# Two loads and two outputs cut in halves, PSUM pairs of any two banks, and new hand lists in a kernel of linear attention and a long convolution

## The chip, the cores and the metric

The kernel runs on one core of a Trainium2 chip. The core has a matrix engine (TensorE, PE in the profile, with its weight loads shown apart as PEld), a vector engine (VectorE, DVE), a scalar engine (ScalarE, ACT), GpSimd (POOL) and SyncE (SP), which here only issues DMAs. Each engine works through its own instructions in order, and waits on semaphores for the others. The accumulator memory PSUM has 8 banks of 512 fp32 numbers per partition. The metric is the device time of one execution in microseconds (us). Before the change three runs took 230.34, 230.67 and 233.8 us, median 230.67 us.

## The reference

The output is two results side by side, 2048 rows of 448 columns each. The left half is linear attention with 16 heads of width 28; the right half is a long convolution, done with Fourier transforms:

```python
# left half
q, k, v = split(x @ wqkv)                         # 2048 x 448 each, 16 heads
phi_q = [softmax(q @ w_phi), softmax(-(q @ w_phi))]   # per head; phi_k the same
kv = phi_k^T @ v;  z = sum(phi_k)
o = (phi_q @ kv) / (phi_q @ z + 1e-6);  a = o @ wo
# right half
K[d, l] = Re sum_n C[d,n] * exp(dt*A[d,n]*l) * dt*B[d,n]     # 448 x 2048, 256 states
y = irfft(rfft(pad(u)) * rfft(pad(K)))[:2048] + u * Dskip
```

## The kernel before, in words

The convolution is made of matrix products. `signal_spectrum(b)` (L417, twice) takes 1024 rows of `u` to the frequency side: it reverses rows with two pairs of matmuls, adds and subtracts on VectorE, and then runs eight groups of eight matmuls against the transform matrix `G1` (L437). Each group fills two PSUM banks, and one copy (L440) takes both banks out in one access. `tables(qt)` (L806) builds, for one quarter `qt` of the 448 channels, the powers of the states: `rotations` are sines on ScalarE, `dampings` are exponentials on ScalarE, both read from a PSUM pair that `args` (four accumulated products of 112 columns) has filled; `hi_tables`, `damp` and `far` are VectorE work; `build_k` (L573) makes the kernel's values with many small matmuls of 80 columns, four steps per bank; `scatter_k` sends them through DRAM. `kernel_spectrum(qt)` (L722) transforms them, and `conv(qt)` (L742) multiplies spectra on VectorE (`prod`), combines them with VectorE (`finish`) or, for two of the eight blocks, with matmuls (`finish_pe`), and `inverse(b, S)` (L781) returns to the time side: for each parity `r` of the rows 36 matmuls of 112 columns into one bank, a copy of 128x448, and a store of 112 KB. 16 such outputs exist.

The attention half is `fold_weights` (L396: `w_phi` folded into the query and key weights, from the loaded block `Wqk`), `key_side`, and `query_side(sc)` (L645) for each 512 rows: logits into four banks, exponentials on ScalarE, the sums, and then 32 matmuls that fill four banks, which two copies of 128x1024 empty (a pair of banks each); four output products of 512 rows follow. The load of `u`, `x`, the state matrices (`Are, Aim, Bre, Cre, Bim, Cim`, 229 KB each) and the weights stands at L283 to L312.

Nothing is scheduled at run time. Every operation is recorded, and four hand lists at the file's end decide all: `ORDER` is the order in which the recorded operations are issued (each engine and each DMA queue keeps that order), `PLACES` gives the SBUF place of each buffer, `SLOTS` the PSUM bank or pair of banks of each job, and `PICKS` the engine of each copy (A is ScalarE, V VectorE) and the queue of each DMA (S is SP's, Q ScalarE's). The semaphore waits are put in when the program is built, from the memory regions that the operations touch.

A pair of banks is read by one access with a stride:

```python
    def two(bs, parts=128):
        return view(psum[0:parts, bs[0], 0:1], [512 * (bs[1] - bs[0]), 2], [1, D_MODEL])
```

All helpers record through one line each, so the profile knows them by these: matmuls L229, PE transposes L239, VectorE tensor operations L186, activations L206 (a new function table is loaded before a sine or an exponential when the other was in use, L203 or L206), copies L214, DMAs L249 and transposing DMAs L245.

Of the kernel before, what the change touches and what calls it, by code (L numbers as in the profile page):

```python
# [17 lines left out]
D_MODEL = 448  # L18
# [111 lines left out]
def kernel(  # L130
# [28 lines left out]
    prog = Prog()  # L159
# [138 lines left out]
    Wqk = sb([112, 4, 2 * D_MODEL])  # L298
    WV = sb([128, 4, D_MODEL])
    dma("S", Wqk, wq3[:, :, 0:2 * D_MODEL])  # L300
# [8 lines left out]
    G1 = sb([128, 2, 4, 512])  # L309
    dma("S", G1, G_d)  # L310
    load_u(0)
# [84 lines left out]
    def fold_weights(which):  # L396
        for cp in range(2):
            p = bank16(*prog.banks(1), [112, 2, D_MODEL])
            c0 = which * D_MODEL + 224 * cp
            transposes([(p[:, k, 112 * j:112 * j + 112], Wqk[:, j, c0 + 112 * k:c0 + 112 * k + 112], id112)  # L400
                        for k in range(2) for j in range(4)])
            copy(wT[:, which, 2 * cp:2 * cp + 2, :], p)
# [14 lines left out]
    def signal_spectrum(b):  # L417
# [9 lines left out]
        for cp in range(2):  # L427
            for st in range(2):
                k = 2 * cp + st
                sg = sb([128, 4, 4, 112])  # L430
                for mp in range(2):
                    items = []
                    bs = prog.banks(2)
                    for k2 in range(2):
                        mt = 2 * mp + k2
                        items += acc(psum[:, bs[k2], 0:D_MODEL],
                                     [(G1[:, cp, jt, 128 * mt:128 * mt + 128], ab[:, cp ^ st, jt, :])  # L437
                                      for jt in range(4)])
                    mms(items)
                    copy(sg[:, :, 2 * mp:2 * mp + 2, :].rearrange("p g k x -> p k g x"),  # L440
                         two(bs).rearrange("p k (g x) -> p k g x", g=4))
# [300 lines left out]
    def conv(qt):  # L742
# [38 lines left out]
        def inverse(b, S):  # L781
            for r in range(2):
                (bk,) = prog.banks(1)
                items = []
                for jt in range(4):
                    items += acc(psum[:, bk, 112 * jt:112 * jt + 112],
                                 [(GI[:, r, cp, mt, 128 * jt:128 * jt + 128], S[:, r, cp, 112 * mt:112 * mt + 112])
                                  for cp in range(2) for mt in range(4)] + [(UT[:, b, r, 128 * jt:128 * jt + 128], DD[:, qt, :])])
                mms(items)
                OB = sb([128, 4, 112])  # L790
                copy(OB.rearrange("p t x -> p (t x)"), psum[:, bk, 0:D_MODEL])
                dma("S", rows(out2, b, r, D_MODEL + 112 * qt), OB)
# [89 lines left out]
).split()]  # L882
PLACES = [64 * int(i) for i in (
# [51 lines left out]
```

## Time and profile before

| | us |
|---|---|
| runs before: lowest, median, highest | 230.34, 230.67, 233.8 |
| the profiled execution, its own time | 231.53 |
| its span (first to last instruction in the trace) | 229.8 |
| TensorE busy | 200.5 (87%) |
| VectorE busy | 211.7 (92%) |
| ScalarE busy | 192.5 (84%) |
| GpSimd busy | 8.0 (3%) |
| mean granted TensorE clock | 0.985 |

The span is the time from the first to the last event on the core; the execution's own time is 1.73 us longer. Busy shares are means over the whole run: in the first ten microseconds the engines wait for loads, in the last eighty ScalarE is no longer full. So the shares are read by stages (a view that gives each engine's busy time in chosen stretches), and the waits beside them. A row of the timeline reads: start, length, engine, line, operation, destination and source with their shapes, how many instructions were joined into the row, and in brackets the idle time before it and what ended it. In the rows of instructions by form the numbers behind the bar are total busy time, the mean of one in nanoseconds, and the idle time before them.

### The profile page before, as it was taken

What the parts mean: (1) busy time and instruction counts of PE and PEld (TensorE: products, weight loads), DVE (VectorE), ACT (ScalarE), POOL (GpSimd) and SP (SyncE); (2) the same over time, 40 slices, a digit from 0 to 9 for tenths busy, and PEclk for the clock granted to TensorE, in tenths of its full rate; (3) what the DMA queues carried; (4) which work ended last, traced back from release to release, by engine and by line L of the source; (5) the groups of instructions that cost most, each with busy time, mean ns of one, the idle gap of its engine ahead of it and who ended that gap; (6) DMA issues with size and microseconds to landing.
All of it is one profiled execution on the core that took longest, in us unless ns stands there. A gap on an engine that the chain in (4) does not pass through costs nothing.

```text
span 229.8 us, 7332 instructions
## 1 busy us (share of the span) xinstructions
PE 200.5 (87%) x3126; PEld 145.6 (63%) x3136; DVE 211.7 (92%) x269; ACT 192.5 (84%) x351; POOL 8.0 (3%) x26
## 2 busy tenths in 40 slices
PE   1154589999999899999887999999999999999993
PEld 1052246655557565787754868565676977799993
DVE  1499999999999899998999999999999989997991
ACT  2799999999999999999999999999798978235320
POOL 2000000001003000020100000010000000000000
PEclk9999599999999999999999999999999999999999
DMA  6992860969638999965576402414949863658842
GB/s 164 187 226 61 239 157 2 222 146 148 163 95 227 196 204 225 170 129 119 179 184 78 161 0 86 161 53 25 289 92 255 276 152 51 73 28 113 232 93 61
DMA packets 77608, 32.87 MB, mean 143 GB/s; under 512 B 64792, under 2 KB 75656, under 8 KB 77192
## 3 DMA queue, kind: packets, MB, share of 16 engines
q1 hardware_dynamic: 69864, 30.11, 60.0%
q10 hardware_dynamic: 7712, 2.31, 5.1%
q8 instruction: 24, 0.39, 0.7%
q14 instruction: 8, 0.07, 0.1%
HBM read 15.84 MB, written 8.49 MB: 106 GB/s over the span
## 4 chain that ended last, share of the span: by engine, by line
ACT 30%; DVE 27%; PE 24%; issue 8%; DMA 8%; DVEq 0%; ACTq 0%
PE psum L229 24%; DVE sbuf L186 24%; ACT sbuf L206 17%; ACT sbuf L214 10%; DMA sbuf<-in_B_C_re_dram 3%; DMA sbuf<-sbuf 2%; DVE sbuf L214 2%; DMA sbuf<-const 2%; DMA sbuf<-in_B_log_dt_dram 1%; ACT L203 1%; ACT L206 1%; ACT sbuf L220 1%; DVE sbuf L198 0%; DVE sbuf L217 0%; DVEq L186 0%
## 5 line engine op out<-in xcount | busy, mean ns | idle before, releaser
L229 PE MATMUL psum<-sbuf 128*128 128x112 bf16 (+9 forms) x3078 | 198.7, 256 | 25.1 <-DVE sbuf L186 12.7
L186 DVE TENSOR_TENSOR sbuf<-sbuf 128x896 bf16<-128x896 bf16 (+13 forms) x214 | 190.2, 947 | 8.9 <-ACT sbuf L206 3.8
L229 PEld LDWEIGHTS <-sbuf 128*128 128x128 bf16 (+5 forms) x3088 | 142.9, 112 | 78.6 <-issue 20.8
L214 ACT CAST sbuf<-psum 128x448 bf16<-128x448 f32 (+6 forms) x122 | 78.6, 701 | 24.8 <-PE psum L229 24.0
L206 ACT ACTIVATE sbuf<-psum 128x512 bf16<-128x512 f32 (+6 forms) x154 | 82.5, 628 | 2.3 <-PE psum L229 1.4
L206 ACT ACTIVATE sbuf<-sbuf 128x896 bf16<-128x896 bf16 (+3 forms) x29 | 18.9, 691 | 2.1 <-DMA sbuf<-in_B_log_dt_dram 1.2
L214 DVE CAST sbuf<-psum 128x448 bf16<-128x448 f32 (+3 forms) x21 | 13.3, 644 | 2.4 <-PE psum L229 2.4
L206 ACT ACTIVATE sbuf<-psum,sbuf 128x896 f32<-128x896 f32 (+3 forms) x17 | 13.9, 833 | 0.0
L224 POOL MEMSET sbuf<- 128x224 bf16 (+7 forms) x21 | 7.6, 397 | 144.0 <-PE psum L229 77.4
L214 ACT COPY sbuf<-psum 112x896 bf16<-112x896 bf16 (+2 forms) x11 | 7.0, 662 | 1.8 <-PE psum L239 1.8
L203 ACT ACT_TABLE_LOAD x5 | 6.4, 1283 | 1.6 <-PEq L919 1.3
L206 ACT ACT_TABLE_LOAD x4 | 5.1, 1283 | 1.8 <-DVE sbuf L186 1.7
L239 PEld LDWEIGHTS <-sbuf 112*112 112x112 bf16 (+1 forms) x48 | 3.1, 120 | 2.0 <-issue 1.7
L239 PE MATMUL psum<-sbuf 112*112 112x112 bf16 (+1 forms) x48 | 3.7, 216 | 0.7 <-DVE sbuf L186 0.6
L186 DVE TENSOR_TENSOR sbuf<-psum,sbuf 128x448 bf16<-128x448 f32 (+1 forms) x6 | 2.9, 489 | 0.6 <-PE psum L229 0.6
L214 DVE CAST sbuf<-sbuf 128x1792 bf16<-128x1792 f32 (+1 forms) x4 | 2.7, 696 | 0.5 <-ACT sbuf L206 0.5
L214 DVE COPY sbuf<-sbuf 128x448 bf16<-128x448 bf16 (+2 forms) x12 | 2.9, 261 | 0.0
L217 DVE TENSOR_SCALAR sbuf<-sbuf 128x1568 bf16<-128x1568 bf16 (+1 forms) x5 | 2.7, 547 | 0.0
L214 ACT COPY sbuf<-sbuf 128x224 bf16<-128x224 bf16 (+2 forms) x6 | 2.5, 424 | 0.0
L220 ACT ACTIVATE sbuf<-sbuf 128x1792 f32<-128x1792 f32 x1 | 1.8, 1795 | 0.0
L198 DVE SCALAR_TENSOR_TENSOR sbuf<-sbuf,psum 128x128 f32<-128x128 f32 x4 | 1.1, 282 | 0.1
L198 DVE SCALAR_TENSOR_TENSOR sbuf<-sbuf 128x896 f32<-128x896 f32 x1 | 1.1, 1079 | 0.0
(8 smaller groups left out, 1.9 us busy)
## 6 DMA issues: line engine op xcount, KB each, us to landing
SUd<-sbuf SPq DMA_DIRECT2D x8, 448.0 KB, 3.6
sbuf<-SUd SPq DMA_DIRECT2D x4, 896.0 KB
sbuf<-const SPq DMA_DIRECT2D x3, 1024.0 KB, 6.0
sbuf<-const SPq DMA_DIRECT2D x8, 384.0 KB, 4.0
sbuf<-in_B_u_dram SPq DMA_DIRECT2D x4, 448.0 KB
out_dram<-sbuf SPq DMA_DIRECT2D x10, 112.0 KB
out_dram<-sbuf SPq DMA_DIRECT2D x2, 448.0 KB, 2.8
out_dram<-sbuf ACTq DMA_DIRECT2D x2, 448.0 KB
```

The source lines that it names most:

```text
L186: prog.add("V", lambda: nc.vector.tensor_tensor(out=o, in0=a, in1=b, op=op))
L198: prog.add("V", lambda: nc.vector.scalar_tensor_tensor(out=o, in0=a, scalar=s, in1=b, op0=op0, op1=op1))
L203: nc.scalar.preload_act_table_set("natural_log_exp_and_others")
L206: nc.scalar.activation(o, a, fn, **kw)
L214: either(lambda: nc.scalar.copy(o, a), lambda: nc.vector.tensor_copy(o, a))
L217: either(lambda: nc.scalar.activation(o, a, ACT.Copy, scale=s), lambda: nc.vector.tensor_scalar_mul(o, a, s))
L220: either(lambda: nc.scalar.activation(o, a, ACT.Square), lambda: nc.vector.tensor_tensor(out=o, in0=a, in1=a, op=ALU.mult))
L224: prog.add("G", lambda: nc.gpsimd.memset(o, v))
L229: nc.tensor.matmul(o, lhsT=l, rhs=r, **kw)
L239: nc.tensor.transpose(o, i, idn)
```

## The change

Three places in the code and all four lists are different.

- The query and key weights `Wqk` are loaded as two tiles with two DMAs of 392 KB, the key part first, in place of one of 784 KB.
- The transform matrix `G1` is loaded as two tiles with two DMAs of 512 KB in place of one of 1024 KB.
- The outputs of the last block (quarter 3, second half of the rows) are made in halves: 18 matmuls, a copy of 128x224 and a store of 56 KB, four times, in place of 36 matmuls, a copy of 128x448 and a store of 112 KB, twice.
- `ORDER`, `PLACES`, `SLOTS` and `PICKS` are new throughout. In `SLOTS` before, all 48 pairs are two neighbouring banks; after, 30 of the 48 are not. 15 copies go from VectorE to ScalarE and 12 from ScalarE to VectorE. Of the six state matrices, `Aim` and `Cim` are now on ScalarE's queue (behind `Are`) and `Cre` on SP's; before, `Cre` was on ScalarE's queue and the others on SP's. The transposing loads of `x` come after the loads of `u`.

```diff
-    Wqk = sb([112, 4, 2 * D_MODEL])
+    Wqk = [sb([112, 4, D_MODEL]) for which in range(2)]
     WV = sb([128, 4, D_MODEL])
-    dma("S", Wqk, wq3[:, :, 0:2 * D_MODEL])
+    for which in (1, 0):
+        dma("S", Wqk[which], wq3[:, :, D_MODEL * which:D_MODEL * which + D_MODEL])
...
-    G1 = sb([128, 2, 4, 512])
-    dma("S", G1, G_d)
+    G1 = [sb([128, 4, 512]) for cp in range(2)]
+    for cp in range(2):
+        dma("S", G1[cp], G_d[:, cp])
...
         def inverse(b, S):
+            n = 2 if (qt, b) == (3, 1) else 4
             for r in range(2):
-                (bk,) = prog.banks(1)
-                items = []
-                for jt in range(4):
...
+                for j0 in range(0, 4, n):
+                    (bk,) = prog.banks(1)
+                    items = []
+                    for jt in range(j0, j0 + n):
...
+                    OB = sb([128, n, 112])
+                    copy(OB.rearrange("p t x -> p (t x)"), psum[:, bk, 0:112 * n])
+                    dma("S", rows(out2, b, r, D_MODEL + 112 * qt)[:, j0:j0 + n], OB)
...
 SLOTS = [[int(c) for c in i] for i in (
-    "67 01 45 23 5 6 7 67 67 23 45 45 67 01 01 67 23 23 45 4 7 23 01 01 45 67 01 01 01 45 45 23 45 67 23 5 0 6 4 1 0 "
+    "67 01 45 23 5 0 7 01 67 27 45 46 04 17 57 12 36 01 24 1 7 35 37 04 57 17 02 13 06 24 01 24 46 36 12 3 4 5 6 5 6 "
...
```

More of the change, by code (lines that the diff above doesn't have):

```diff
@@ L398, in fold_weights @@
             p = bank16(*prog.banks(1), [112, 2, D_MODEL])
-            c0 = which * D_MODEL + 224 * cp
-            transposes([(p[:, k, 112 * j:112 * j + 112], Wqk[:, j, c0 + 112 * k:c0 + 112 * k + 112], id112)
+            c0 = 224 * cp
+            transposes([(p[:, k, 112 * j:112 * j + 112], Wqk[which][:, j, c0 + 112 * k:c0 + 112 * k + 112], id112)
                         for k in range(2) for j in range(4)])
@@ L436, in signal_spectrum @@
                         items += acc(psum[:, bs[k2], 0:D_MODEL],
-                                     [(G1[:, cp, jt, 128 * mt:128 * mt + 128], ab[:, cp ^ st, jt, :])
+                                     [(G1[cp][:, jt, 128 * mt:128 * mt + 128], ab[:, cp ^ st, jt, :])
                                       for jt in range(4)])
@@ L781, in inverse @@
         def inverse(b, S):
+            n = 2 if (qt, b) == (3, 1) else 4
             for r in range(2):
-                (bk,) = prog.banks(1)
-                items = []
-                for jt in range(4):
[L786 to L792, printed above, removed]
+                for j0 in range(0, 4, n):
+                    (bk,) = prog.banks(1)
+                    items = []
+                    for jt in range(j0, j0 + n):
+                        items += acc(psum[:, bk, 112 * (jt - j0):112 * (jt - j0) + 112],
+                                     [(GI[:, r, cp, mt, 128 * jt:128 * jt + 128], S[:, r, cp, 112 * mt:112 * mt + 112])
+                                      for cp in range(2) for mt in range(4)]
+                                     + [(UT[:, b, r, 128 * jt:128 * jt + 128], DD[:, qt, :])])
+                    mms(items)
+                    OB = sb([128, n, 112])
+                    copy(OB.rearrange("p t x -> p (t x)"), psum[:, bk, 0:112 * n])
+                    dma("S", rows(out2, b, r, D_MODEL + 112 * qt)[:, j0:j0 + n], OB)
         ta = sb([128, 2, 2, 896])
@@ L844 @@
 ORDER = [int(i) for i in (
[37 rows of a table removed]
[38 rows of a table added]
 ).split()]
 PLACES = [64 * int(i) for i in (
[12 rows of a table removed]
[12 rows of a table added]
 ).split()]
 SLOTS = [[int(c) for c in i] for i in (
[4 rows of a table removed]
[5 rows of a table added]
 ).split()]
 PICKS = (
-    "SSQSSSSSSSSSSSSSSSVAVVVAAAVAVAAAAAAAAASAASAASAASAAAAAAAAASAASAASAASSSSSSSSSVVAVVAAAASSSSSSSSAAAAAAAA"
-    "AAAAAAAAVAAVSSSSVVAVVAAAASSSSSSSSSSSSSSSSAVAAAAAAASVVAAAAAASSAAAAAAVAASSAQAQAAAQASVVVVVVAAASQSSSSSSA"
-    "VAAAAVAAAAAAAAAVQSASASAAASASVVAAAAAVASSSSQQSQAAAVVVAAVVAAVVAAAQSVQASAQVSVAAAAAAASASASAQVS"
+    "SQSSQSSSSSSSSSSSSSSSAAVVVAAAVAVAAAAAAAAASAASAASAASAAAAAAAAASAASAASAASSSSSSSSSVVAVVAAAASSSSSSSSAAAAAA"
+    "AAAAAAAAAAVVAASSSSVVAVVAAAASSSSSSSSSSSSSSSSAVAAAAAAASVVAAAAAASSAAAAAAAAAQSASAQAAVQAQVVVAVAAVVSSSSSSS"
+    "SAAAAVAAVAAAAAVAAVSSASASAAASASVVAAVAVVVQSSQSSSQAAAAAAAVAVAAAVAAVQSAQASAQASVAAAAAAASAQAQAQASAQVQ"
 )
```

106 rows, old and new, of tables (ORDER, PLACES, SLOTS) are left out of this document.

## The prediction

> **What bounds the kernel now.** First the page's busy line and the shares of the chain that ended last:
>
> ```profile
> PE 200.5 (87%) x3126; PEld 145.6 (63%) x3136; DVE 211.7 (92%) x269; ACT 192.5 (84%) x351; POOL 8.0 (3%) x26
> ACT 30%; DVE 27%; PE 24%; issue 8%; DMA 8%; DVEq 0%; ACTq 0%
> ```
>
> No engine has the chain to itself, so I read busy time by stages (us:us, stage length, then each engine's busy time, the granted clock, DMA share):
>
> ```profile
> 28.00:60.00 32.00, 30.33 (x211) 17.45 (x210) 32.00 (x47) 31.86 (x46) 1.10 (x3) 0.98 0.64 132
> 62.00:143.00 81.00, 76.19 (x1331) 54.90 (x1339) 79.14 (x102) 79.89 (x171) 4.78 (x11) 1.00 0.69 151
> 140.00:152.50 12.50, 12.12 (x313) 8.76 (x312) 12.47 (x20) 12.38 (x22) 0.66 (x3) 1.00 0.33 113
> 152.50:226.30 73.80, 73.19 (x1309) 58.94 (x1308) 69.06 (x82) 46.71 (x90) 0.00 (x0) 1.00 0.66 137
> ```
>
> From 28 to 143 VectorE and ScalarE are full (ScalarE idles 0.14 and 1.11 us), so time lost by ScalarE there cannot be caught up. From 152.5, where `finish_pe` of quarter 0 begins, TensorE is full to the end: 73.19 of 73.8 us. In the changed program the same TensorE operations stand behind that point, so the end follows the start of `finish_pe` by this much, whatever the others do. Three times matter, then: when VectorE and ScalarE get going, whether they stay full to 143, and when TensorE reaches `finish_pe`. The chain and timeline for the head and the tail:
>
> ```profile
> 3.74 6.80 DMA sbuf<-in_B_C_re_dram
> 3.74 0.20 ACT L206 ACTIVATE sbuf<-sbuf 112x4 bf16<-112x4 bf16 x1 [1.20 <-DMA sbuf<-in_B_log_dt_dram]
> 10.64 0.69 DVE L186 TENSOR_TENSOR sbuf<-sbuf 112x1024 bf16<-112x1024 bf16 x1 [2.50 <-DMA sbuf<-in_B_C_re_dram]
> 11.97 1.28 ACT L206 ACT_TABLE_LOAD   x1 [1.72 <-DVE sbuf L186]
> ...
> 224.57 0.62 DVE L214 CAST sbuf<-psum 128x448 bf16<-128x448 f32 x1 [1.01 <-PE psum L229]
> 226.34 0.53 ACT L214 CAST sbuf<-psum 128x448 bf16<-128x448 f32 x1 [4.02 <-PE psum L229]
> 226.90 0.38 ACTq L249 DMA_DIRECT2D out_dram<-sbuf  x1
> ```
>
> **The change part by part.** All is summed against the profiled run (231.53 us, span 229.8); the difference is then put on the median, 230.67.
>
> *Loads at the head.* `Cre` waits on ScalarE's queue behind the exponential of the step sizes and lands at 10.54; VectorE has idled 2.50 us by then and ScalarE 1.72. After, `Cre` goes third on SP, `Cim` takes its place behind the exponential, and the transposing loads of `x` come later. The wait cannot fall by more than 2.50, nor below nothing if `Cim` lands as late as `Cre` did. All six state matrices are 1.4 MB; before, 6.80 us also held the first `x` loads. I take 1.9 us for VectorE and, since ScalarE's sine table waits for VectorE's fourth operation there, **-1.7** for ScalarE (0 to -2.5).
>
> The Trainium skill, "Trainium Kernel Development and Optimization", section "Key Constraints", says that DMAs from all queues share 16 DMA engines and that issuing from several engines saves only issue time. By that the move would be worth the 0.4 us of an issue, and the sum below would be 1.3 us higher. This trace has one order only and cannot decide it.
>
> *Loads in two parts.* The DMA rows (issue; KB each, us from issue to landing):
>
> ```profile
> 21.10 0.36 SPq L249 DMA_DIRECT2D sbuf<-const  x1
> sbuf<-const SPq DMA_DIRECT2D x3, 1024.0 KB, 6.0
> ```
>
> One more issue of 0.36 us for each, the bytes are the same. `G1` lands near 27.1 and is first used at 29.1 (row below), when VectorE releases it. I cost the parts at nothing: TensorE's reversing matmuls cover them. If the first half landed late, the groups would lose what they gain at the head, 1.7 us, no more.
>
> *Copies moved.* 15 to ScalarE, 12 to VectorE; the rows for a plain copy:
>
> ```profile
> L214 ACT CAST sbuf<-psum 128x448 bf16<-128x448 f32 x69 | 37.1, 568 | 22.9 <-PE psum L229 22.2 <-ACT sbuf L214 0.5
> L214 DVE CAST sbuf<-psum 128x448 bf16<-128x448 f32 x17 | 10.4, 620 | 2.4 <-PE psum L229 2.4
> L214 ACT CAST sbuf<-psum 128x896 bf16<-128x896 f32 x27 | 24.3, 993 | 0.8 <-PE psum L229 0.8
> L206 ACT ACTIVATE sbuf<-psum 128x896 bf16<-128x896 f32 x12 | 11.9, 992 | 0.0
> ```
>
> VectorE loses about 1.6 us in all, ScalarE gains 1.5, mostly late, where it idles; up to the numerators of `query_side(1)` at 143 ScalarE has **+0.6** more to do.
>
> *Pairs of any banks.* This is the part that decides. A pair of banks 1 and 3 is one access with a stride, and the waits that the changed program carries treat bank 2 between them as touched. I compared each wait with the bytes really shared: before, no wait between TensorE and ScalarE lacks a true overlap; after, some 18 do. They fall in two chains.
>
> First chain, 28 to 60 us: the `G1` groups. Eight matmuls fill a pair, a copy empties it:
>
> ```profile
> 29.10 4.84 PE L229 MATMUL psum<-sbuf 128*128 128x448 bf16 x24 [0.20 <-DVE sbuf L186]
> 31.30 3.10 ACT L206 ACTIVATE sbuf<-psum 128x896 bf16<-128x896 f32 x6
> 34.23 2.59 ACT L214 CAST sbuf<-psum 128x896 bf16<-128x896 f32 x3
> ```
>
> A group is 4.84 / 3 = 1.6 us, a copy 0.8 back to back, and before, groups run ahead of copies. With a false wait a group starts only after a copy (or damping exponential) of another pair, and ScalarE, which needs that group next or next but one, idles for 1.6 us plus 0.2 for the handover, less the ScalarE work in between. Walking the new order with these lengths from the last reversing copy on, I find six such places: behind the copies of `signal_spectrum(1)`'s first four groups and the damping of quarter 1, 0.5 + 1.3 + 1.7; where a copy waits for half a group that fills the bank between, 1.65; and around `fold_weights(0)`'s second half, 1.0 + 0.7. Together 6.85 us; before, ScalarE lost 0.14. The two smallest are no longer than a handover's error, so I count half of them: **+6.2** (0, if ScalarE is ahead of need, to 8). Of that, ScalarE's idle time of 62 to 143 can give back **-1.1** (0 to 3: VectorE idles 1.86 us there and TensorE 4.8, so some busy time may be waiting that shrinks).
>
> Second chain, 143 to 152.5, on the way to `finish_pe`:
>
> ```profile
> 143.59 7.99 PE L229 MATMUL psum<-sbuf 28*32 28x512 bf16 x171
> 144.16 1.93 ACT L214 CAST sbuf<-psum 128x1024 bf16<-128x1024 f32 x2
> 146.11 1.28 ACT L206 ACT_TABLE_LOAD   x1
> 147.40 1.17 ACT L206 ACTIVATE sbuf<-psum 128x224 bf16<-128x224 f32 x2
> 148.45 0.54 ACT L214 CAST sbuf<-psum 128x448 bf16<-128x448 f32 x1
> 148.86 1.03 ACT L206 ACTIVATE sbuf<-psum,sbuf 128x896 bf16<-128x896 f32 x1
> 151.86 0.81 PE L229 MATMUL psum<-sbuf 128*128 128x512 bf16 x2 [0.28 <-DVE sbuf L214]
> ```
>
> Before, TensorE never stops here: while ScalarE empties the numerators' banks (1.93), loads the sine table and makes rotations(3), TensorE does `build_k(2)`, `args`, output products and `query_side(2)`'s logits. After, the third step of `build_k(2)` (bank 3) waits for both copies of 128x1024, since the second one's pair reaches over bank 3: 1.9 us of TensorE idle. Everything on TensorE queues behind it: `args` of rotations(3), so the table and the sines come later; then the logits wait for the sine that spans their bank (table 1.28, two sines 1.17, a copy 0.54: 3.0; only 1.7 if the table is loaded early), and the output products wait for a VectorE copy of `build_k` and another sine (0.6 + 1.0). That is 5.2 to 6.5 us of idle. Before, TensorE idled 0.4 us of the 12.5, which goes into these. I take the lower end less that, **+4.9** (0, if the copies run far ahead, to 6.5).
>
> *Last outputs in halves.* The nearest row to the copy of 128x224, though from SBUF:
>
> ```profile
> L214 ACT COPY sbuf<-sbuf 128x224 bf16<-128x224 bf16 x4 | 1.7, 416 | 0.0
> ```
>
> The last copy of 448 columns takes 0.53 us, so 0.1 is gained. The store that follows carries half the bytes: **-0.2** (0 to -0.4; the two extra instructions lie beside matmuls). *Tail:* TensorE idles 0.6 us of 73.8, and some short waits hide in its busy time; **-1.0** if they close, which I take (0 to -1.0), as the other engines have had longer.
>
> Sum: -1.7 + 0.6 + 6.2 - 1.1 + 4.9 - 1.0 - 0.2 = +7.7 us; 230.67 + 7.7 = **238.4 us**, 3.3% slower.
>
> **The rivals.**
>
> (a) *The false waits cost nothing and the head's gain comes through.* If both chains fall where the waiting engine had something else to wait for, -1.7 - 0.2 remain: **228.8 us**. For it: VectorE is full in 28 to 143, and if it alone paces, the others' idle time is free. Against it: ScalarE is as full (31.86 of 32), and TensorE's 73.8 us start only after the second chain. It decides for faster if `finish_pe` starts before 152.5. The Trainium skill, "PSUM — Partial Sum Buffer", section "PSUM bank collisions raise a hardware error", asks for a guard by bank and quadrant of partitions. By that rule a copy of banks 1 and 3 owes bank 2 nothing, and the sum would be this rival's. The program's waits are stricter than that rule; before, all pairs are neighbours, so its trace shows neither.
>
> (b) *Only the second chain bites.* If the `G1` groups' lateness is caught up by 143 (VectorE pacing, ScalarE's instructions shrinking by 3 us and more), -1.7 + 0.6 + 4.9 - 0.5 - 0.2 = +3.1: **233.8 us**.
>
> (c) *VectorE loses as well.* The product of `conv(0)`, which waits for `args` of rotations(3), and the `build_k` copy that waits for a sine each stop VectorE for about 3 us in the second chain, and VectorE has 69.06 us of the last 73.8 to do: it is then late at the end by the part that 4.7 us of slack does not cover, and in the first chain by what the late copies hold up. That adds 3 to 4 us: **242 us**.
>
> That the two-part loads let the first `G1` groups start earlier, as they are meant to, is part of (a): they have no wait on the load to lose.
>
> **How the numbers follow.** The forecast, both chains paying, 235.5 to 240.5 us: 0.42. (b), 231.5 to 235.5: 0.25. (a), 226 to 231.5: 0.18. (c): 0.15. 2% is 4.6 us, about what can be told from no change: the band is 226.1 to 235.3. Faster by over 2% would need all of the head's gain (2.5) and more than 2 us elsewhere, 0.04. Within 2%: nearly all of (a) and of (b), 0.38. Slower by over 2%: the rest, 0.58. The range leaves out a tenth on each side: half of (a) below, the upper half of (c) above: **229 to 242.5 us**. It covers both ends of the head (0 to -2.5) and, each by itself, of the chains (0 to 8, 0 to 6.5). Of both signs slower holds most, and its own range is 233 to 242.5.
>
> **What would show it.** Head: VectorE's wait of 2.50 us at 10.64 shrinks below 1. First chain: ScalarE's busy time in 28 to 60 falls to about 26 of 32 us, with rows of copies and dampings that name TensorE as releaser, and TensorE's idle time there names ScalarE's L214. Second chain: TensorE's first 28*32 matmuls end, then two copies of 128x1024, then 80-column matmuls of L229 that were waiting for L214; TensorE busy some 7 us of 13 before `finish_pe`, which starts near 160. Tail: again about 73 us of full TensorE. The forecast is wrong if ScalarE stays full in 28 to 60, or if TensorE's work before `finish_pe` has no gap; then (a) or (b) holds.

## The result and the profile after

The changed kernel takes 252.04 us (median, 251.65 to 253.68) against 230.77 us before: a ratio of 1.094, with a 95% interval of 1.088 to 1.100. It was forecast slower, at 238.4 us with 242.5 as the upper end; the loss is 21.3 us in place of 7.7.

The page of the kernel after, its busy line and the first shares of its chain:

```profile
PE 205.6 (82%) x3126; PEld 148.4 (59%) x3136; DVE 212.4 (85%) x267; ACT 195.6 (78%) x355; POOL 8.0 (3%) x26
...
PE 62%; ACT 26%; DMA 5%; issue 3%; DVE 2%; ACTq 0%; DVEq 0%
```

Busy times have hardly grown (TensorE 200.5 to 205.6, VectorE 211.7 to 212.4, ScalarE 192.5 to 195.6 us); the shares have fallen because the span has grown by 20.4 us. So it is waiting, not work. By stages (stage, length, busy time of TensorE, weight loads, VectorE, ScalarE, GpSimd, granted clock, DMA share and rate):

```profile
28.00:60.00 32.00, 26.12 (x160) 14.50 (x159) 28.40 (x43) 25.11 (x35) 1.50 (x5) 0.93 0.52 114
62.00:143.00 81.00, 70.16 (x1094) 48.82 (x1098) 68.74 (x87) 72.40 (x150) 3.75 (x8) 0.96 0.71 150
158.00:173.00 15.00, 9.20 (x203) 6.12 (x178) 11.13 (x13) 10.50 (x16) 0.51 (x2) 1.00 0.17 53
172.70:247.00 74.30, 73.38 (x1308) 59.06 (x1308) 67.46 (x80) 46.55 (x91) 0.00 (x0) 1.00 0.67 132
```

ScalarE, which had 31.86 of 32 us before, has 25.11 in 28 to 60, and 72.40 of 81 where it had 79.89. From 172.7, where `finish_pe` of quarter 0 begins (152.5 before), TensorE is full again to the last matmul: the whole loss is made before that point. Five rows of the view of waits, summed over the run (engine, line, what it waited for: us, times, longest):

```profile
ACT sbuf L214 <- PE psum L229: 29.9, 28, 5.1
PE psum L229 <- ACT sbuf L214: 16.5, 11, 3.3
DVE sbuf L186 <- ACT sbuf L206: 13.2, 7, 4.2
PE psum L229 <- ACT sbuf L206: 10.2, 10, 1.9
ACT sbuf L206 <- PE psum L229: 7.8, 11, 2.5
```

The second row was 7.5 us in 6 times before and the last one 1.4; TensorE waiting for L206 was not among the ten largest then. TensorE and ScalarE wait for each other in turn. TensorE's rows with idle time ahead of them, in the timeline (start, length, how many; in brackets the idle time and what ended it), show where:

```profile
36.41 1.67 PE L229 MATMUL psum<-sbuf 128*128 128x448 bf16 x8 [0.99 <-ACT sbuf L214]
45.34 1.67 PE L229 MATMUL psum<-sbuf 128*128 128x448 bf16 x8 [1.14 <-ACT sbuf L214]
48.83 1.49 PE L229 MATMUL psum<-sbuf 128*128 128x448 bf16 x7 [1.81 <-ACT sbuf L206]
57.08 2.24 PE L229 MATMUL psum<-sbuf 128*128 128x448 bf16 x11 [1.64 <-ACT sbuf L214]
64.13 2.05 PE L229 MATMUL psum<-sbuf 128*128 128x448 bf16 x10 [1.45 <-ACT sbuf L214]
...
108.81 1.01 PE L229 MATMUL psum<-sbuf 128*112 128x116 bf16 x16 [1.00 <-ACT sbuf L206]
110.82 1.47 PE L229 MATMUL psum<-sbuf 128*128 128x32 bf16 x23 [1.00 <-ACT sbuf L206]
138.70 1.28 PE L229 MATMUL psum<-sbuf 128*128 128x112 bf16 x12 [3.31 <-ACT sbuf L214]
...
160.35 2.62 PE L229 MATMUL psum<-sbuf 128*32 128x80 bf16 x88 [2.09 <-ACT sbuf L214]
164.66 4.00 PE L229 MATMUL psum<-sbuf 128*128 128x512 bf16 x75 [1.69 <-ACT sbuf L206]
170.57 2.73 PE L229 MATMUL psum<-sbuf 128*128 128x448 bf16 x12 [1.91 <-ACT sbuf L206]
```

Each of these eleven rows begins with an operation that waits for an access of ScalarE with which it shares no byte, but whose pair reaches over its bank. In the built programs TensorE has 19 such waits on ScalarE after the change (the prediction said some 18) and none before. The first five are the first chain of the prediction, the last three the second. The three at 109, 111 and 139 us are a chain of their own: matmuls of `key_side` around two exponentials of `dampings(2)`, and a step of `kernel_spectrum(0)` behind the copies of 128x1024 of `query_side(0)`. Compared with their own times before: the group before `fold_weights` ends 7.2 us late near 65, the numerators of `query_side(1)` start 14.2 us late at 157.6, `finish_pe` starts 20.2 us late at 172.7.

### The profile page after: what moved, and what is told of

Same layout as the page of the kernel before. It is cut to its first block, busy times and chain, and to the rows that moved or that the text cites. A ratio compares the mean times of both kernels' runs of the same rounds, so it can differ in the third digit from the quotient of the medians.

```text
span 250.2 us, 7318 instructions
## 1 busy us (share of the span) xinstructions
PE 205.6 (82%) x3126; PEld 148.4 (59%) x3136; DVE 212.4 (85%) x267; ACT 195.6 (78%) x355; POOL 8.0 (3%) x26
## 4 chain that ended last, share of the span: by engine, by line
PE 62%; ACT 26%; DMA 5%; issue 3%; DVE 2%; ACTq 0%; DVEq 0%
PE psum L229 61%; ACT sbuf L206 15%; ACT sbuf L214 11%; DMA sbuf<-in_B_C_im_dram 2%; DMA sbuf<-sbuf 2%; DVE sbuf L186 2%; DMA sbuf<-in_B_log_dt_dram 1%; ACT L203 1%; DVE sbuf L214 1%; PE psum L239 0%; ACTq L214 0%; DVEq L214 0%; ACTq L206 0%; DVEq L186 0%
## 5 line engine op out<-in xcount | busy, mean ns | idle before, releaser
L229 PE MATMUL psum<-sbuf 128*128 128x112 bf16 (+10 forms) x3078 | 203.7, 258 | 41.0 <-ACT sbuf L214 16.5
L186 DVE TENSOR_TENSOR sbuf<-sbuf 128x896 bf16<-128x896 bf16 (+12 forms) x214 | 191.7, 949 | 19.4 <-ACT sbuf L206 13.2
L229 PEld LDWEIGHTS <-sbuf 128*128 128x128 bf16 (+6 forms) x3088 | 145.7, 113 | 97.0 <-issue 40.7
L214 ACT CAST sbuf<-psum 128x448 bf16<-128x448 f32 (+7 forms) x124 | 78.8, 681 | 35.6 <-PE psum L229 29.9
L206 ACT ACTIVATE sbuf<-psum 128x512 bf16<-128x512 f32 (+6 forms) x154 | 83.2, 622 | 8.0 <-PE psum L229 7.8
L206 ACT ACTIVATE sbuf<-sbuf 128x896 bf16<-128x896 bf16 (+3 forms) x29 | 18.9, 693 | 2.5 <-DVE sbuf L186 1.7
L214 DVE CAST sbuf<-psum 128x448 bf16<-128x448 f32 (+4 forms) x21 | 12.5, 611 | 8.4 <-PE psum L229 8.4
L206 ACT ACTIVATE sbuf<-psum,sbuf 128x896 f32<-128x896 f32 (+3 forms) x17 | 13.6, 821 | 1.0 <-DVE sbuf L214 0.9
L217 DVE TENSOR_SCALAR sbuf<-sbuf 128x1568 bf16<-128x1568 bf16 x4 | 2.5, 617 | 0.0
L214 ACT COPY sbuf<-sbuf 128x224 bf16<-128x224 bf16 (+1 forms) x6 | 2.3, 381 | 0.0
L217 ACT ACTIVATE sbuf<-sbuf 112x448 bf16<-112x448 bf16 x1 | 0.6, 577 | 0.8 <-DVE sbuf L309 0.8
```

The lines of the kernel that those rows point to most:

```text
L186: prog.add("V", lambda: nc.vector.tensor_tensor(out=o, in0=a, in1=b, op=op))
L206: nc.scalar.activation(o, a, fn, **kw)
L214: either(lambda: nc.scalar.copy(o, a), lambda: nc.vector.tensor_copy(o, a))
L217: either(lambda: nc.scalar.activation(o, a, ACT.Copy, scale=s), lambda: nc.vector.tensor_scalar_mul(o, a, s))
L229: nc.tensor.matmul(o, lhsT=l, rhs=r, **kw)
```

## The experiments

Theory 1: the waits on banks between the two of a pair make the loss. Rivals: the new order and the copies that changed engine are slow by themselves; the late stages only hand on the lateness of the first; or an access to banks apart takes longer itself.

**Banks of a pair neighbours again, nothing else.** Only `SLOTS` of the changed kernel is replaced:

```diff
-    "67 01 45 23 5 0 7 01 67 27 45 46 04 17 57 12 36 01 24 1 7 35 37 04 57 17 02 13 06 24 01 24 46 36 12 3 4 5 6 5 6 "
+    "56 01 23 45 7 0 0 23 45 67 23 67 45 67 23 67 01 23 67 1 2 01 45 01 23 23 01 01 34 67 23 56 23 45 67 7 5 2 0 7 "
...
```

> The changed kernel with one list altered: SLOTS, in which all 48 pairs are neighbouring banks again; order, places, picks, loads and outputs are those of the change. Theory 1 (waits on banks between the two of a pair make the 20 us): the time falls back to 228 to 233 us, TensorE's gaps that end with ScalarE's copies at 36, 45, 49, 57, 64, 139, 160, 165 and 171 us go. Rival (the new order and the copies that changed engine are slow by themselves): it stays above 245 us.

Measured: 237.19 us, ratio 1.021 (1.015 to 1.027). The first `G1` group starts at 26.7 us in place of 29.1, and the last of the first chain is 2.2 us earlier than before the change, not 7.2 later. 15 of 21 us are gone with one list. The rest, 4 us above the upper end of what was expected, is put down to new true conflicts that this choice of neighbours brought (TensorE stops 1.92 us at 81, 1.1 us at 109); the second choice of neighbours, below, bears that out for the most part.

**The other way round: the kernel before with its banks renamed.** No work, order or true conflict changes, only the distance of the two banks of a pair.

The first lines of `SLOTS` of the two, beside that of before:

```diff
-    "67 01 45 23 5 6 7 67 67 23 45 45 67 01 01 67 23 23 45 4 7 23 01 01 45 67 01 01 01 45 45 23 45 67 23 5 0 6 4 1 0 "
+    "57 02 46 13 6 5 7 57 57 13 46 46 57 02 02 57 13 13 46 4 7 13 02 02 46 57 02 02 02 46 46 13 46 57 13 6 0 5 4 2 0 "
+    "37 04 26 15 6 3 7 37 37 15 26 26 37 04 04 37 15 15 26 2 7 15 04 04 26 37 04 04 04 26 26 15 26 37 15 6 0 3 2 4 0 "
...
```

> The kernel before with its banks renamed (1 and 2 exchanged, 5 and 6 exchanged): 38 of 48 pairs then lie one bank apart, all else is as before. Theory 1: slower by 5 to 25 us, with gaps of TensorE before G1 groups and build_k steps. Rival: 230 to 232 us, since no work, order or true conflict is altered.

> The kernel before with banks renamed so that all 48 pairs are two to four banks apart (01 becomes 04, 23 becomes 15, 45 becomes 26, 67 becomes 37). Theory 1: slower than the renaming with one bank between, by more than 10 us against before, since each pair now covers two or three foreign banks. Rival: 230 to 232 us.

Measured: 244.25 us, ratio 1.054 (1.049 to 1.059), and 281.0 us, ratio 1.213 (1.206 to 1.220). A renaming of banks alone costs 13 and 49 us. TensorE's waits for ScalarE in the second of the two (1.1 and 7.5 us before the renaming), and its copies of a pair:

```profile
PE psum L229 <- ACT sbuf L206: 24.5, 13, 5.1
PE psum L229 <- ACT sbuf L214: 23.0, 17, 5.0
...
L214 ACT CAST sbuf<-psum 128x896 bf16<-128x896 f32 x27 | 24.0, 909 | 20.6 <-PE psum L229 20.1 <-issue 0.5
```

A copy of a pair three or four banks apart takes 909 ns in the mean, one of neighbours 993 before. So the access itself is not slower, and the last rival falls; what has grown is the waiting ahead of it.

**One chain at a time.** In the changed kernel some accesses to pairs apart are made as two instructions, one per bank, so that neither touches what lies between:

```diff
+            for o_, a_ in banks_apart(i, o, a):     # [(o[:, 0], a[:, 0]), (o[:, 1], a[:, 1])] for the chosen ones
+                nc.scalar.activation(o_, a_, fn, **kw)
```

Second chain (two copies of 128x1024, two sines):

> The changed kernel, in which only the two copies of 128x1024 of query_side(1) and the two sines of rotations(3) that read pairs apart are made as two instructions each, one per bank (4 instructions more, nothing else altered). Theory 1: TensorE's three gaps at 160, 165 and 171 us (2.1, 1.7, 1.9 us) go, the additional instructions cost 0.2 us each: 252 falls to 246 to 248 us. Rival: no change beyond 1 us.

First chain (20 accesses before 66 us):

> The changed kernel, in which the accesses to pairs apart in the first 66 us (G1 groups, reversing copies, fold_weights, sines and exponentials of quarters 0 and 1) are made as two instructions, one per bank: 20 more instructions of ScalarE, nothing else altered. Theory 1: the first chain's gaps go, which with neighbouring banks moved the stage's end from 7.3 us late to 2.2 us early; 20 instructions of 0.2 us cost ScalarE some 4 us. 252 falls to 245 to 248 us. Rival (the order is slow): 252 or more.

The middle (two exponentials, two copies):

> The changed kernel, in which only two exponentials of dampings(2) and the two copies of 128x1024 of query_side(0) are made as two instructions each, one per bank (4 more). Theory 1 with a third chain, left out of the prediction: TensorE's gaps at 109, 111 and 139 us (1.0, 1.0, 3.3 us) go, 252 falls to 246 to 249 us. Rival (the middle stage only hands on the first chain's lateness): above 250.5 us.

All 33:

> The changed kernel, in which all 33 accesses to pairs apart are made as two instructions, one per bank; order, places, picks and banks are those of the change. Theory 1: the whole 20 us go but for what 33 more instructions of ScalarE cost (0.2 us each, most of it while ScalarE is full): 231 to 238 us. Rival: above 245 us.

Measured: 244.61, 243.40, 246.36 and 232.08 us. Against 252.04 the runs gain 7.4 (second chain), 8.6 (first) and 5.7 us (middle), each net of its additional instructions; together 21.7. The changed kernel was not run again beside them, and the kernel before took 231.54 and 231.99 us there in place of 230.77, so each gain may be about 1 us larger. With all 33 split the ratio to before is 1.003 (0.999 to 1.007): nothing is left of the loss, in the same order and with the same banks. ScalarE is full again in the two stages in which it had lost:

```profile
28.00:60.00 32.00, 30.19 (x205) 17.18 (x204) 31.91 (x46) 31.92 (x61) 1.82 (x5) 1.00 0.72 151
62.00:143.00 81.00, 76.09 (x1332) 54.69 (x1330) 78.03 (x107) 80.29 (x177) 3.96 (x9) 1.00 0.67 143
```

The rival of the slow order falls, and so does the one of lateness handed on: the middle is worth 5.7 us while the first chain still is there.

The profiled executions say the same. `finish_pe` starts at 165.5, 164.1, 166.6 and 152.5 us in place of 172.7. In the first of these 1.5 of the 7.3 us lie ahead of the numerators (156.1 in place of 157.6), where its program is still that of the change; from there to `finish_pe` it takes 9.4 in place of 15.1 us. So 5.8 us are the second chain's own, and the rest of its 7.4 is not.

The first and the second chain each gave some 1.5 us more than was expected of them. For the first one reason is that an additional instruction costs less than the 0.2 us put in: ScalarE is busy 196.0 us with all 33 split and 194.0 in the second run with neighbours below, 0.06 us for each. Three copies of pairs in the latter, and the same three as six instructions in the former:

```profile
32.95 2.58 ACT L214 CAST sbuf<-psum 128x896 bf16<-128x896 f32 x3
33.32 2.78 ACT L226 CAST sbuf<-psum 128x448 bf16<-128x448 f32 x6
```

**Without the additional instructions.**

> The changed kernel with neighbouring pairs for all that starts in the first 70 us (SLOTS alone), the change's own banks after it, and there the 12 accesses to pairs apart made as two instructions, one per bank. Theory 1: neither the waits of the change nor the new conflicts of the first run (TensorE gaps of 1.9 us at 81, 1.1 at 109) are left, and the head's gain of 2 us comes through less 12 instructions: 228.5 to 232 us. If the new order itself is the slower one by the 6 us that the neighbouring banks left: 235 to 238 us.

> The changed kernel with SLOTS alone altered: all 48 pairs neighbouring banks, chosen so that no job needs a bank before its last reader is done by the times of the run with 33 accesses made as two (which left few late ones in the first choice of neighbours: 6 us). Theory 1: no waits on foreign banks, no new conflicts and no additional instructions, so the run with all accesses in two (232.1 us) less some 3 us of instructions: 227.5 to 230.5 us, faster than before. Rival (the new order is as good as the old one and no better): 231 to 233 us.

Measured: 231.97 us, ratio 1.001 (0.997 to 1.005), for neighbours in the first 70 us and 12 accesses in two after them; 233.32 us, ratio 1.007 (1.003 to 1.011), for neighbours throughout, chosen by the times of the run with all 33 in two. The first lies at the upper end of what was expected. The second does not: it was to take 227.5 to 230.5 us, or 231 to 233 by its rival, and is 0.7% slower than the kernel before, though the two stops of the first choice at 81 and 109 us are down to 0.4 and 0.6 us, and 4 of the 6 us are gone with them. Neither is faster than the kernel before: of the new order, freed of its waits, no gain is left to see.

**`G1` by one load.** On the second choice of neighbours:

```diff
-    for cp in range(2):
-        dma("S", G1[cp], G_d[:, cp])
+    dma("S", view(G1[0], [G1[1].offset - G1[0].offset, 2], [1, 2048]), G_d.rearrange("p c j m -> p c (j m)"))
```

> The kernel with neighbouring pairs throughout (second choice), in which G1 comes by one DMA of 1024 KB in place of two of 512 KB, in the place of the first in SP's queue. If the parts matter, the first G1 groups wait for the load at 27 us and the time rises by 0.5 to 2 us; the prediction's reading (cost and gain nothing): within 0.7 us.

Measured: 231.35 us, ratio to before 0.999 (0.995 to 1.002). Neither expectation holds: one load is 2.0 us faster than two (231.35 for 233.32), and not slower or the same. The first group starts at 26.8 or 26.9 us in both, so it is not the load's own landing. In the profiled executions, 1.0 us apart, TensorE with two parts lost 0.8 us in 180 to 200 (18.89 busy against 19.72), far from the load. One DMA less shifts which older DMA each later one waits for; that this is the cause was not tested.

**The head alone.** The kernel before with only the loads of the state matrices (and the first load of `x`) in the order of the change:

```diff
-    "30 35 0 3 41 1 2 5 6 42 44 43 7 67 45 8 61 9 59 49 52 58 50 53 54 10 62 60 51 37 75 4 57 46 "
+    "30 35 0 3 5 7 6 9 41 1 2 8 42 44 43 67 45 61 59 49 52 58 50 53 54 62 60 51 37 75 4 57 10 46 "
...
-    "SSQSSSSSSSS"
+    "SQSSQSSSSSS"
```

> The kernel before with its own lists and banks, in which only the loads at the head are those of the change: Aim and Cim on ScalarE's queue, Cre on SP's, the first transposing load of x behind the first load of u. Prediction's term: VectorE's first product of state matrices starts near 8.7 to 9.3 in place of 10.64 us and the whole is faster by 1 to 2 us: 229.5 to 231 against 231.5. Rival (all queues share the DMA engines, so moving a load wins only its issue): within 0.5 us.

Measured: 232.74 us, ratio 1.003 (1.000 to 1.007), so neither the gain nor the time within 0.5 us that the rival named. The timeline of this kernel:

```profile
10.51 1.28 ACT L206 ACT_TABLE_LOAD   x1
...
113.03 1.17 PE L229 MATMUL psum<-sbuf 128*128 128x8 bf16 x36 [2.16 <-DMA sbuf<-sbuf]
```

The sine table is loaded at 10.51 in place of 11.97 us, so the head does gain 1.5 us, and at 104 us VectorE is still 1.1 us ahead. At 113 TensorE then waits 2.16 us for the copies of the key-value block, where it waited 0.24 us for ScalarE before: these four DMAs came no earlier, since the last two wait for two loads of transform tables. In this execution the gain ends there.

> The kernel before with the loads at the head of the change, as in the run of the head alone, and with two of the eight 384 KB loads of transform tables (those of tiles 4 and 7) issued on SP behind the four small copies of the key-value block in place of ahead of them. There the head alone had ScalarE and VectorE 1.1 us early at 104 us and lost it at 113 us, where TensorE waited 2.16 us for the key-value copies, of which the last two wait for these two loads. If that is where the head's gain went, the wait at 113 falls below 0.7 us and the whole is faster than the kernel before by 0.7 to 1.5 us; if the gain is lost elsewhere as well, within 0.5 us of it.

In `ORDER`, beside the change of the head, the loads 490 and 493 (transform tables) are moved behind 397, the last of the key-value copies 400, 399, 398, 397.

Measured: 232.84 us, ratio 1.003 (1.001 to 1.006). The wait at 113 is gone, and still there is no gain: this expectation failed too. The profiled execution, the slowest of its twelve (233.71 us), cannot tell why. ScalarE had lost 1.2 us at 34 already: the groups of 448 columns ran at half pace for 4 us, as told in the last section. They did not do so in the run of the head alone, whose program is the same up to there. At 100 us TensorE waited 0.8 us for a DMA, and the sine table there was loaded at 105.3 us, 2.2 us later than in the kernel before. What the head's gain is worth is thus left open; it does not show in the whole time in either.

## Why the prediction was right and wrong

**Right: the bound, the mechanism and the sign.** The end follows the start of `finish_pe` by 74.5 us (73.8 before), and pairs apart make the waits: renaming banks alone costs 13 to 49 us, splitting the accesses takes the whole loss away. The signs named for the head and the first chain came: VectorE's wait fell from 2.50 to 0.43 us, and ScalarE has 25.11 of 32 us in 28 to 60 ("about 26"). By the guard by bank and quadrant (the Trainium skill, "PSUM — Partial Sum Buffer", section "PSUM bank collisions raise a hardware error") a copy of banks 1 and 3 owes bank 2 nothing. No run here has the change's own accesses without those waits; the nearest to it, all 33 accesses in two, ran at 232.08 us, not at the 228.8 of rival (a).

**The sum, stage by stage.** In its trace the changed kernel is late by 7.2 us near 65 us, by 14.2 at the numerators, by 20.2 at `finish_pe` and by 20.4 at the end: +7.2, +7.0, +6.0 and +0.2. The forecast had for these stretches +5.1 (-1.7 + 0.6 + 6.2), -1.1, +4.9 and -1.2 (-1.0 - 0.2). Of the 12.7 us that it lacks, 8.1 lie in the second stretch.

**Wrong: the step that failed is the -1.1 us for 62 to 143.** I listed some 18 false waits and let them "fall in two chains", and booked the middle as time given back. There is a third chain: TensorE's gaps of 1.0, 1.0 and 3.3 us at 109, 111 and 139, and what ScalarE and VectorE lost with them. Split in two, its four accesses are worth 5.7 us in the whole time, an error of 6.8; three such waits stand in this stretch, and the sum gave them no price. Nothing was given back: ScalarE had 72.40 of 81 us.

**Mis-sized: the first chain, +6.2, measured 8.6 us**, and that net of 20 additional instructions. I priced the stalls from ScalarE's side and began at the last reversing copy. The chain begins earlier: a reversing matmul waits for a sine and the `args` of the dampings (products of 224 columns, not of 112) for a copy at 26 and 28 us,

```profile
25.97 0.53 PE L229 MATMUL psum<-sbuf 128*128 128x448 bf16 x1 [0.98 <-ACT sbuf L206]
27.82 6.47 PE L229 MATMUL psum<-sbuf 128*128 128x224 bf16 x26 [1.32 <-ACT sbuf L214]
```

and these two take what the head had won before `G1` starts: its first group begins at 29.1 us as before, and at 26.7 or 26.8 where these waits are gone.

**Mis-sized, by less: the second chain, +4.9, measured 5.8 to 6.0.** The three gaps came where I put them: behind both copies of 128x1024, behind the table and a sine, behind VectorE's copy and another sine. I had 5.2 to 6.5 us and took the lower end. `finish_pe` starts 14.5 us after the end of the numerators, against 8.5 before: +6.0 in the trace, and splitting its accesses took 5.8 out of this stretch. VectorE stops there too, as rival (c) has it (1.56 us at 163, 2.20 at 169), but TensorE is full from `finish_pe` on as before, so no run shows that VectorE's loss reached the end.

**The head, -1.7:** near its size at its place, as two rows of the kernel after show, VectorE 1.4 (for 1.9) and ScalarE's table 1.4 us early (for 1.7).

```profile
9.23 0.69 DVE L186 TENSOR_TENSOR sbuf<-sbuf 112x1024 bf16<-112x1024 bf16 x1 [0.43 <-DMA sbuf<-in_B_C_im_dram]
10.57 1.28 ACT L206 ACT_TABLE_LOAD   x1 [0.17 <-DVE sbuf L186]
```

That is more than the 0.4 us of an issue. It does not contradict the rule of the Trainium skill, "Trainium Kernel Development and Optimization", section "Key Constraints", that issuing from several engines saves only issue time: the order of the loads changed as well, and no run here changes the queue alone. But the term should not have been added to the sum as if it reached the end. The kernel before with this head alone is no faster.

**The tail, -1.0 and -0.2:** TensorE's stage did not close up (74.5 for 73.8). From its last matmul to the end of the span it is 3.0 us in place of 3.5, so the halves gave 0.5. The last copies of 224 columns take 0.34 us on ScalarE, less than the 0.42 that the row from SBUF gave:

```profile
247.24 0.34 ACT L214 CAST sbuf<-psum 128x224 bf16<-128x224 f32 x1 [0.46 <-PE psum L229]
```

**The range:** its upper end was 242.5 because the two chains were bounded by 8 and 6.5 us each, the middle was given no loss at all, and the head was taken as won. With the three runs at 8.6, 5.7 and 7.4 the sum is 21.7.

**Loads in parts, copies moved:** at the place where `G1` is used its parts cost and gain nothing, as forecast; in the whole time two parts were 0.8% slower than one, for a reason not settled. The parts of `Wqk` and the moved copies were not tested by themselves; with all 33 accesses split, together with the rest of the change, they leave no difference.

## What to carry to other kernels

Where one strided access reads two PSUM banks, the waits of a program like this one cover the banks between them as well, so keep the banks of a pair neighbours, or read them one by one, which cost ScalarE 0.06 us for each here. When a list of waits has been made, price every one on it in its own stage; a wait left out of the sum is a forecast of nothing, and three bottlenecks that pass a baton add up almost fully (by the start of `finish_pe` 8.6, 6.1 and 7.3 us alone, 20.2 with all 33 accesses split). A gain at the head is not to be booked at the end before each stage behind it has been shown to hand it on.

## What the hardware showed that I had not expected

After some gaps TensorE's matmuls of 448 columns come at 0.37 us in place of 0.19, for a time that differs from run to run. The weight loads of two kernels with the same program up to that point, first the one with the key-value copies moved, then the head alone:

```profile
28.48 0.14 PEld L229 LDWEIGHTS <-sbuf 128*128 128x128 bf16 x2 [1.57 <-issue]
28.84 0.15 PEld L229 LDWEIGHTS <-sbuf 128*128 128x128 bf16 x1 [0.22 <-issue]
29.21 0.15 PEld L229 LDWEIGHTS <-sbuf 128*128 128x128 bf16 x1 [0.22 <-issue]
29.59 0.15 PEld L229 LDWEIGHTS <-sbuf 128*128 128x128 bf16 x1 [0.22 <-issue]
```

```profile
25.75 1.27 PEld L229 LDWEIGHTS <-sbuf 128*128 128x128 bf16 x7 [0.22 <-issue]
28.45 5.61 PEld L229 LDWEIGHTS <-sbuf 128*128 128x128 bf16 x31 [1.43 <-issue]
```

In the first the steps of 0.37 us last to 32.9, in the second loads follow each other at 0.18 from 28.45 on. The changed kernel has 7 such slow steps from 29.6 to 32.2 us, 1.3 us in all, on top of its waits. The Trainium skill, "TensorE: Matmul & The Clock Gate", section "Part 1: The HAM clock gate (the "warmup" mystery)", has a clock of half speed until the engine has been busy for some 3.4 us; by it 448 columns would take an estimated 0.37 us at half clock, which agrees. The column of the granted clock (the third number from the end of a row by stages) shows it in some traces and not in others. Its rows for the changed kernel, around these steps and behind its wait of 3.31 us at 138.7; then the head alone and the first kernel above in 24 to 28, where both have steps of 0.37 up to 25.6; and the first kernel's slow stretch:

```profile
28.00:33.00 5.00, 5.00 (x21) 2.57 (x20) 5.00 (x11) 4.96 (x8) 0.00 (x0) 0.58 0.89 110
138.60:141.50 2.90, 2.58 (x16) 1.72 (x17) 1.71 (x3) 0.55 (x2) 0.00 (x0) 0.51 0.01 1
...
24.00:28.00 4.00, 3.04 (x12) 1.62 (x11) 4.00 (x5) 4.00 (x7) 0.00 (x0) 0.61 1.01 215
24.00:28.00 4.00, 3.15 (x12) 1.62 (x11) 4.00 (x5) 4.00 (x7) 0.00 (x0) 1.00 0.95 219
28.00:33.00 5.00, 4.49 (x13) 1.86 (x14) 5.00 (x9) 4.82 (x8) 0.00 (x0) 1.00 0.64 147
```

The last row reads 1.00 for a stretch in which 13 matmuls took the time of 24. The low readings agree with the pace of the rows, and the two readings of 1.00 do not: there the pace of the rows is to be trusted. A gap made by a wait can thus cost twice, as at 138.7 us: once as a gap, and once more in the matmuls behind it. How much of the whole loss this second cost is, no run separates.
